# Opening loads in one queue, a second attention and turn bank, and earlier due times for batch 1

## The chip, the cores and the metric

One core of a Trainium2 chip. TensorE (PE) multiplies, VectorE (DVE) and ScalarE (ACT) work element by element, GpSimd (POOL) and SyncE (SP) issue loads and stores here. The metric is device time in microseconds, median of the runs.

## The reference

Linear attention with the map phi(x) = elu(x) + 1, then a mixture of four dense experts with given probabilities, over 8 batches of 8 heads, 576 rows and 64 channels (4608 tokens of 512 channels, 1024 hidden).

```python
q_p, k_p = (phi(q), phi(k))
kv = np.einsum('bhsd,bhse->bhde', k_p, v)
z = np.sum(k_p, axis=2)
num = np.einsum('bhsd,bhde->bhse', q_p, kv)
den = np.einsum('bhsd,bhd->bhs', q_p, z)[..., None] + 1e-06
...
p = domain_probs / (domain_probs.sum(-1, keepdims=True) + 1e-09)
for e in range(E):
    h = np.maximum(x @ w1[e], 0.0)
    out += p[:, e:e + 1] * (h @ w2[e])
```

## The kernel before, in words

**Tiles.** Heads are taken in pairs (two heads of 64 channels fill 128 partitions), four pairs per batch. Of a batch's 576 rows the first 512 are its main block (four chunks of 128); the last 64, the rests, of two batches share 128 partitions. After attention, x of the 512 main rows is one block j = 0 to 7; the rests of all batches make block 8.

**Attention of one pair** (`attention`, L302): k and q are mapped by an Exp on ACT (L332) and two operations on DVE (L324, L325), v is cast on ACT (L328). PE turns q with the identity (L342, and L345 for the rests' part) into the bank `tbank` (l2b3); ACT copies the turned q out (L353), DVE its rests' part (L355). PE forms key times value over the main rows (L364) and the rests (L367) into the bank `at`, ACT copies it (L377, L378), PE multiplies it with the turned q (L388), first three chunks, then the fourth and the rests, both in `at`, and DVE divides each by its denominator (L399, L401, L408). So a pair needs the mapped rests (`rest_maps`, L280: Exp L292, cast L295, DVE L289 and L290), once per batch. For batch 0, PE also turns x (`turn_x`, L485, into l2b3) and DVE copies it (L490). From batch 2 on the turns are DMA transposes issued by SP (L358).

**Experts.** Block 0 is done plainly: `first_l1` (L495: 32 products of 512 columns per expert) and `first_l2` (L505: 32 more). Expert 0's first layer is the wide form: six of the eight columns of hidden units are summed in six banks (l1b0 to 2, l2b0 to 2) as each pair's x arrives, the other two after. The other 64 units (8 blocks x 2 halves x 4 experts) use seven products of quarter blocks in place of eight (L649 and L757; expert 3's first layer is plain, L705). For that, sums of weight quarters are formed on DVE once (`sums_w1` L445, `sums_w2` L468), and each unit's scaled x (ACT, L607) is turned by a DMA transpose of SP (L609).

**Loads.** POOL issues pairs 1 to 3 of batch 0, all of batch 1 and the 32 weight loads (fp32 in HBM, cast to fp16 on the way), in program order. SP issues pair 0 and the rests of batch 0, the probabilities, and everything from batch 2 on. The pairs of batches 0 and 1 have three stage buffers in turn (two of their own, and w and m2, which the units use later); so pair (1,3) is loaded where pair (1,0) was.

**Order.** Every step is handed to a planner (`Plan`, L21) with engine, assumed duration, due time, keys that it reads and writes, and for loads an assumed transfer time (`move`). `order` (L55) plays the steps through: of those that are ready on the engine that is free first, the one with the earliest due time goes next; POOL keeps program order; a step is ready `HOP` after what it depends on. The result is the fixed order of instructions on each engine: on the chip each engine waits at the head of its own list, whatever is ready behind it. The planner's keys only set the order; waits on the chip follow from the tiles. A due time of a unit is `U(n)` = 84 + 6.4 n; batch 1's pairs are due at 47, 56, 65 and 72 (L847 to L858).

Of the kernel before, what the change touches and what calls it, by code (L numbers as in the profile page):

```python
# [20 lines left out]
class Plan:  # L21
# [6 lines left out]
    HOP = 0.2  # L28
# [7 lines left out]
    def add(self, eng, dur, pri, fn, r=(), w=(), move=0.0, after=0.0):  # L36
        n = len(self.ops)
        deps = set()
        for key in r:
            if key in self.wr:  # L40
                deps.add(self.wr[key])
            self.rd.setdefault(key, []).append(n)
        for key in w:
            if key in self.wr:
                deps.add(self.wr[key])
            deps.update(x for x in self.rd.get(key, ()) if x != n)
        for key in w:
            self.wr[key] = n
            self.rd[key] = []
        self.ops.append(  # L50
            dict(eng=eng, dur=dur, pri=pri, fn=fn, deps=deps, move=move, after=after)
        )
        return n
# [56 lines left out]
def kernel(  # L110
# [94 lines left out]

    def stage_keys(i):
# [6 lines left out]
    def dma(queue, pri, out_, in_, w, move, r=()):  # L213
        eng = nc.gpsimd if queue == "POOL" else nc.sync
        pl.add(
            queue,
            0.7 if queue == "POOL" else 0.45,
            pri,
            lambda: eng.dma_start(out=out_, in_=in_),
            r=r,  # L220
            w=w,
# [5 lines left out]
    def load_pair(b, pr, queue, pri):  # L227
# [5 lines left out]
        for t, o, key in ((k, kqs[i][:, 0], kk[0]), (v, vss[i], kk[2]), (q, kqs[i][:, 1], kk[1])):  # L233
            dma(queue, pri, o, t[b, hs, 0:NT].rearrange("h (p c) d -> p h c d", c=C), (key,), 0.82)

    def load_rest(b, queue, pri):
        par = b % 2
        rs = slice(par * R, par * R + R)
        for i, (t, o) in enumerate(((k, kqr[rs, 0]), (v, vr[rs]), (q, kqr[rs, 1]))):
            dma(queue, pri, o, t[b, :, NT:S].rearrange("h s d -> s h d"), (("str", par, i),), 0.6)  # L240

    def load_w1(e, dcs):
        for dc in dcs:
            dma("POOL", 0, w1_sb[e][:, dc, :], moe_w1[e, dc * P : (dc + 1) * P, :],
                (("w1", e, dc // 2, 0), ("w1", e, dc // 2, 1), ("w1c", e, dc)), 1.5)

    def load_w2(e):
        src = moe_w2[e].rearrange("(f p) d -> p f d", p=P)
        for c in range(0, FC, 2):
            i = c // HF  # L250
            dma("POOL", 0, w2_sb[e][:, c : c + 2, :], src[:, c : c + 2, :],
                (("w2", e, i, 0), ("w2", e, i, 1), ("w2c", e, c // 2)), 1.5)


    def probs():
# [24 lines left out]
    def rest_maps(b, pe_mode, pri):  # L280
# [7 lines left out]
        def maps():  # L288
            nc.vector.tensor_scalar(kqpr[rs], kqr[rs], 0.0, 1.0, AO.max, AO.add)  # L289
            nc.vector.tensor_tensor(out=kqpr[rs], in0=er[rs], in1=kqpr[rs], op=AO.min)  # L290

        pl.add("ACT", 1.15, pri, lambda: nc.scalar.activation(er[rs], kqr[rs], AF.Exp),  # L292
               r=(s_[0], s_[2]), w=ek)
        pl.add("ACT", 0.65, pri + 0.1,
               lambda: nc.scalar.copy(vprs[par][rs, :, 0:D], vr[rs]), r=(s_[1],), w=(("vpr", par),))  # L295
        pl.add("DVE", 1.8, pri + 0.5, maps, r=(s_[0], s_[2]) + ek, w=("kpr", "qpr"))
# [5 lines left out]
    def attention(b, pr, pe_mode, pri, step):  # L302
# [28 lines left out]
        for i in order_:  # L331
            pl.add("ACT", 0.65, pri + i * step, lambda i=i: nc.scalar.activation(  # L332
# [3 lines left out]
            if i == 0:  # L336
                pl.add("ACT", 0.62, pri + step, vcast, r=(sk[2],), w=(("vp", vi),))
        if pe_mode:

            def turn():  # L340
                for c in range(C):
                    nc.tensor.transpose(  # L342
                        out=tbank[:, c * P : (c + 1) * P], in_=qp[:, c], identity=identh
                    )
                nc.tensor.transpose(  # L345
                    out=tbank[:, NT : NT + R],
# [28 lines left out]
        def kvcopy():  # L375
            pkv = slot[0].rearrange("p (h e) -> p h e", h=2)
# [4 lines left out]
               r=(("kqp", pi, 0), ("vp", vi), ("vpr", par), "kpr"), w=("at",))  # L381
        pl.add("ACT", 0.45, pri + 4.5 * step, kvcopy, r=("at",), w=(("kvz", zi),))
# [13 lines left out]
        def norm(c0, n, ri):  # L396
            nd = at[:, 0 : n * 2 * DE].rearrange("p (c h e) -> p c h e", c=n, h=2)
# [17 lines left out]
        for u, (c0, n) in enumerate(((0, 3), (3, 2))):  # L415
            ri = rot("rc", 2)
            pl.add("PE", 0.06 * n, pri + (5 + u) * step, lambda c0=c0, n=n: nd_mm(c0, n),
                   r=(("qT", ti), ("qTr", par, pr), ("kvz", zi)), w=("at",))
            pl.add("DVE", (0.72, 0.75)[u], pri + (5.5 + u) * step,
                   lambda c0=c0, n=n, ri=ri: norm(c0, n, ri), r=("at",),  # L420
# [14 lines left out]

    def sums_w1(e, pri):
# [4 lines left out]
        K = lambda i, kk: ("w1", e, kk, i)  # L441
# [6 lines left out]
        for o, a, b_, alu, r, w in (  # L448
            (w1x[e][:, 2], q00, q01, AO.add, (K(0, 0), K(0, 1)), (X(2),)),
            (w1x[e][:, 1], q10, q11, AO.add, (K(1, 0), K(1, 1)), (X(1),)),  # L450
            (w1x[e][:, 0], q00, q11, AO.add, (K(0, 0), K(1, 1)), (X(0),)),
            (q10, q10, q00, AO.subtract, (K(0, 0),), (K(1, 0),)),
            (q01, q01, q11, AO.subtract, (K(1, 1),), (K(0, 1),)),
        ):
            pl.add("DVE", 0.75, pri, two(o, a, b_, alu), r=r, w=w)
        pl.add("DVE", 0.4, pri, lambda: nc.vector.tensor_scalar(q00, q00, -1.0, None, AO.mult),
               r=(), w=(K(0, 0),))

    def sums_w2(e, pri):
# [3 lines left out]
        K = lambda i, j: ("w2", e, i, j)  # L463
# [7 lines left out]
        for o, a, b_, r, w in (  # L471
            (t[0], qd(0, 1), qd(0, 0), (K(0, 1), K(0, 0)), T(0)),
            (t[1], qd(1, 1), t[0], (K(1, 1), T(0)), T(1)),
            (t[2], qd(1, 1), qd(0, 1), (K(1, 1), K(0, 1)), T(2)),
            (qd(0, 1), qd(1, 0), t[1], (K(1, 0), T(1)), K(0, 1)),
        ):
            pl.add("DVE", 0.75, pri, two(o, a, b_), r=r, w=(w,))


    def turn_x(pr, pri):  # L480
# [9 lines left out]
        pl.add("DVE", 0.45, pri + 0.5, lambda: nc.vector.tensor_copy(xt0[:, pr, :], tbank[:, 0:NT]),  # L490
# [22 lines left out]
    def w1k(e, dc, fj):  # L513
        return (("w1", e, dc // 2, fj // HF), ("w1c", e, dc))

    def w2k(e, fj):
        return (("w2", e, fj // HF, 0), ("w2", e, fj // HF, 1), ("w2c", e, fj // 2))

    def first_l1(e, pri, step, wide):
        ht = []  # L520
        banks = [(l1b[i], ("l1b%d" % i)) for i in range(3)]
        if wide:
            banks += [(l2b[i], ("l2b%d" % i)) for i in range(3)]
        ht = [rot("ht", len(hts)) for _ in range(FC)]

        def relu(fj, bank, key, pr_):
            pl.add("ACT", 0.6, pr_, lambda: nc.scalar.activation(hts[ht[fj]], bank, AF.Relu),
# [3 lines left out]
        if wide:  # L531
            for dc in range(DC):
                for fj in range(6):
                    bank, key = banks[fj]
                    p_ = pri + (dc * 6 + fj) * step
# [5 lines left out]
            done = 6  # L541
# [14 lines left out]
    def first_l2(e, ht, pri, step, wide):  # L556
# [17 lines left out]
        for i, (c, fjs, bi) in enumerate(parts):  # L574
            bank, key = l2b[bi], "l2b%d" % bi
# [4 lines left out]
            pl.add("PE", 0.216 * len(fjs), p_,  # L580
                   lambda c=c, fjs=fjs, bank=bank: mm2(e, ht, c, fjs, bank), r=r, w=(key,))
            if fjs[-1] == FC - 1:
                pl.add("DVE", 0.69, p_ + 1.0, lambda c=c, bank=bank: post(c, bank),
                       r=(key, "pnat"), w=(("ot", c // 2, c % 2),))
# [8 lines left out]
    def prep(n):  # L593
# [5 lines left out]
        for c in range(2):  # L599
# [7 lines left out]
            pl.add("ACT", 0.65, pri, lambda c=c, src=src, ps=ps: nc.scalar.activation(  # L607
# [23 lines left out]
    def l1_seven(n):  # L631
# [11 lines left out]
        K = lambda i, kk: ("w1", e, kk, i)  # L643
        X = lambda i: ("w1x", e, i)

        def prod(bank, wt, r, start):
# [14 lines left out]
            (A, ka, w1x[e][:, 2], X(2), xT[:, 1, 2:4], t_, True),  # L661
            (Bk, kb, w1x[e][:, 1], X(1), xT[:, 0, 0:2], t_, True),
# [268 lines left out]
```

## Time and profile before

| | us |
|---|---|
| median of 3 runs | 562.05 (557.68 to 563.96) |
| the profiled execution | 562.97 |
| its span in the profile | 561.2 |
| PE busy | 498.4 (89%) |
| DVE busy | 413.5 (74%) |
| ACT busy | 335.7 (60%) |
| POOL busy | 38.9 (7%) |

How to read the rows below. A stretch row has its bounds, its length, then the busy time of PE, PEld (TensorE's loads of the stationary operand, beside PE), DVE, ACT and POOL with the number of instructions, the mean granted clock of TensorE (1.00 is full speed), the mean busy share of the 16 DMA engines and the GB/s moved. A timeline row has the start, the length, the engine, the line of the kernel and the operation, what it writes and reads, its shape and the count merged into it; in brackets the idle time of the engine ahead of it and what ended that. SPq and POOL rows with DMA_DIRECT2D are issues of loads, not transfers. A wait row has the waiting engine and line, what ended the wait, the total, the number and the longest.

### The profile page before, as it was taken

The page shows a single profiled execution, that of the slowest core. Times are in us where ns is not written, and L with a number is a line of the kernel's source. Part 1 is how long each engine was busy: PE and PEld are TensorE (multiplying, and loading weights), DVE is VectorE, ACT ScalarE, POOL GpSimd, SP SyncE. Part 2 cuts the span into 40 slices and gives each one's busy share as a digit, 9 for nine tenths or more (in the row PEclk, how much of TensorE's full clock was granted, in tenths as well). Part 3 has the DMA queues.
Part 4 walks back from the last instruction along what each step waited for, and adds up shares of the span by engine and source line. Part 5 has one row for each costly group of instructions (what it writes and reads, how often), then busy time and mean ns, then how long its engine had stood idle before and what let it go on. Part 6 is the DMA issues. An engine that isn't in the chain of part 4 may idle for free.

```text
span 561.2 us, 13887 instructions
## 1 busy us (share of the span) xinstructions
PE 498.4 (89%) x5624; PEld 427.8 (76%) x5624; DVE 413.5 (74%) x993; ACT 335.7 (60%) x617; POOL 38.9 (7%) x62
## 2 busy tenths in 40 slices
PE   0067979578999999999999999999999999999994
PEld 0033434235899999999999999999999999999993
DVE  2175565847969888988888898889897775757662
ACT  2143345488547965895687678756854674656431
POOL 7545030000000000000000000000000000000000
PEclk9998998889999999999999999999999999999998
DMA  9999328398535745693668447564434242523211
GB/s 226 231 216 233 73 73 143 110 201 180 144 48 148 167 107 143 116 219 69 127 146 170 112 112 147 146 138 119 86 68 86 39 95 43 92 39 77 39 40 39
DMA packets 126929, 67.44 MB, mean 120 GB/s; under 512 B 97520, under 2 KB 120816, under 8 KB 126864
## 3 DMA queue, kind: packets, MB, share of 16 engines
q1 hardware_dynamic: 118384, 52.26, 43.0%
q0 software_dynamic: 8480, 14.29, 12.2%
q8 instruction: 44, 0.72, 0.5%
q14 instruction: 21, 0.17, 0.1%
HBM read 45.16 MB, written 9.44 MB: 97 GB/s over the span
## 4 chain that ended last, share of the span: by engine, by line
PE 83%; DVE 6%; DMA 6%; ACT 2%; issue 2%; POOL 1%; DVEq 0%; ACTq 0%; POOLq 0%
PE l2b L757 33%; PE l1b L649 25%; PE l1b L705 10%; PE l1b L495 6%; DMA w<-in_moe_w_dram 5%; PE l2b L505 3%; PE at L388 2%; PE at L364 1%; DVE x L401 1%; DVE ot L562 1%; DMA xT<-xp 1%; PE l2b L495 1%; DVE rc L399 1%; DVE kqp L324 1%; DVE kqp L325 0%
## 5 line engine op out<-in xcount | busy, mean ns | idle before, releaser
L649 PE MATMUL l1b<-xs,w 128*128 128x128 f16 x1536 | 114.8, 219 | 1.5 <-ACT h L686 0.9
L757 PE MATMUL l2b<-w,h 128*128 128x256 f16 x768 | 112.3, 273 | 0.8 <-DVE h L693 0.8
L757 PE MATMUL l2b<-t,s 128*128 128x256 f16 x768 | 111.1, 273 | 0.0
L649 PEld LDWEIGHTS <-w 128*128 128x128 f16 x1536 | 99.6, 98 | 5.4 <-issue 1.8
L757 PEld LDWEIGHTS <-s 128*128 128x128 f16 x1024 | 93.6, 98 | 8.1
L607 ACT ACTIVATE xp<-x,p_nat 128x512 f16<-128x512 f16 x112 | 75.2, 716 | 7.5 <-DMA xT<-xp 7.2
L649 PEld LDWEIGHTS <-w1x 128*128 128x128 f16 x1152 | 74.9, 98 | 4.6 <-issue 2.0
L757 PEld LDWEIGHTS <-h 128*128 128x128 f16 x768 | 69.9, 98 | 7.1 <-DVE h L693 1.1
L705 PE MATMUL l1b<-xT,w 128*128 128x256 f16 x512 | 74.2, 273 | 0.0
L743 DVE TENSOR_TENSOR s<-h 128x512 f16<-128x512 f16 x128 | 53.7, 420 | 26.7 <-ACT h L724 26.2
L724 ACT ACTIVATE h<-l1b 128x512 f16<-128x512 f32 x64 | 38.2, 596 | 43.2 <-PE l1b L705 35.6
L649 PE MATMUL l1b<-xT,w1x 128*128 128x128 f16 x768 | 57.6, 219 | 0.0
L625 DVE TENSOR_TENSOR xs<-xT 128x256 f16<-128x256 f16 x144 | 49.2, 375 | 9.9 <-PE l1b L649 5.9
L705 PEld LDWEIGHTS <-w 128*128 128x128 f16 x512 | 49.6, 98 | 5.6
L683 ACT ACTIVATE h<-l1b 128x512 f16<-128x512 f32 x48 | 28.6, 596 | 33.7 <-PE l1b L649 33.3
L332 ACT ACTIVATE ek<-kq 128x512 f16<-128x512 f32 x60 | 37.3, 627 | 14.2 <-DVE kqpr L290 7.4
L689 DVE CUSTOM_DVE_ANT_0 h<-l1b,w 128x512 f16<-128x512 f32 x48 | 33.0, 687 | 16.2 <-PE l1b L649 7.8
L675 ACT ACTIVATE l1b<-l1b 128x512 f32<-128x512 f32 x48 | 28.0, 583 | 23.6 <-PE l1b L649 20.2
L757 PE MATMUL l2b<-w,s 128*128 128x256 f16 x256 | 38.4, 273 | 0.0
L680 DVE TENSOR_TENSOR w<-l1b,m 128x512 f32<-128x512 f32 x48 | 33.0, 687 | 7.2 <-PE l1b L649 4.7
L324 DVE TENSOR_SCALAR kqp<-kq 128x512 f16<-128x512 f32 x60 | 25.5, 424 | 15.8 <-PE at L364 11.8
L693 DVE CUSTOM_DVE_ANT_0 h<-l1b,w 128x512 f16<-128x512 f32 x48 | 33.0, 689 | 4.1 <-PE l1b L649 2.2
(89 smaller groups left out, 627.3 us busy)
## 6 DMA issues: line engine op xcount, KB each, us to landing
w<-in_moe_w_dram POOLq DMA_DIRECT2D x32, 256.0 KB, 8.9
out_dram<-ot SPq DMA_DIRECT2D x16, 512.0 KB, 2.9
kq<-in_k_dram SPq DMA_DIRECT2D x25, 256.0 KB, 3.2
vs<-in_v_dram SPq DMA_DIRECT2D x25, 256.0 KB, 3.1
kq<-in_q_dram SPq DMA_DIRECT2D x25, 256.0 KB, 3.1
kq<-in_k_dram POOLq DMA_DIRECT2D x5, 256.0 KB, 8.0
vs<-in_v_dram POOLq DMA_DIRECT2D x5, 256.0 KB, 8.0
kq<-in_q_dram POOLq DMA_DIRECT2D x5, 256.0 KB, 7.4
```

The costliest lines, as they stand in the source:

```text
L332: pl.add("ACT", 0.65, pri + i * step, lambda i=i: nc.scalar.activation(ek[:, i], kq[:, i], AF.Exp), r=(sk[i],), w=(("ek", ei, i),))
L495: nc.tensor.matmul(out=bank, lhsT=w1_sb[e][:, dc, fj * P : (fj + 1) * P], rhs=xt0[:, dc, :], start=(dc == 0), stop=(dc == DC - 1),)
L607: pl.add("ACT", 0.65, pri, lambda c=c, src=src, ps=ps: nc.scalar.activation(xp[:, c, :], src, AF.Copy, scale=ps), r=r, w=(("xp", xi, c),))
L625: lambda o=o, a=a, b_=b_, alu=alu: tt(out=o, in0=a, in1=b_, op=alu),
L649: nc.tensor.matmul(out=bank[:, fc * P : (fc + 1) * P], lhsT=wt[:, kc, fc * P : (fc + 1) * P], rhs=r[:, kc, :], start=(start and fc == 0 an ...
L680: pl.add("DVE", 0.69, p_ + 1.5, lambda: nc.vector.tensor_tensor(out=w, in0=W, in1=m2_b, op=AO.subtract), r=(kw, ("m2",)), w=(("w", wi),))
L689: pl.add("DVE", 0.69, p_ + 0.5, lambda: nc.vector._custom_dve(TENSOR_ADD_SAT, out=hq(n, 1, 1), in0=A, in1=w, s0=BIG, s1=0.0), r=(ka, ("w", ...
L693: pl.add("DVE", 0.69, p_ + 0.5, lambda: nc.vector._custom_dve(TENSOR_ADD_SAT, out=hq(n, 0, 0), in0=Bk, in1=w, s0=BIG, s1=0.0), r=(kb, ("w" ...
L705: nc.tensor.matmul(out=ph[:, f2 * 2 * P : (f2 + 1) * 2 * P], lhsT=w1_sb[e][:, dc, (2 * fp + f2) * P : (2 * fp + f2 + 1) * P], rhs=xT[:, :, ...
L724: lambda ph=ph, f=f, c0=c0: nc.scalar.activation(h[:, :, f, c0 : c0 + 2, :], ph.rearrange("p (c u t) -> p u c t", c=2, u=2), AF.Relu), r=( ...
L743: pl.add("DVE", 0.42, U(n + 1) + d - 0.5, lambda i=i, a=a, b_=b_, alu=alu: tt(out=s4[:, i], in0=a, in1=b_, op=alu), r=r, w=(Q(i),))
L757: nc.tensor.matmul(out=l2b[bank][:, half * HD : (half + 1) * HD], lhsT=a[:, c, :], rhs=w[:, c], start=(opens and first and c == 0), stop=( ...
```

## The change

The diff, cut to what changes the order of work (durations of other steps are set 0.07 to 0.13 lower throughout; reads and writes of weight slices are named per slice loaded instead of per pair of slices):

- The rests of batch 0 are loaded by POOL, ahead of its other loads; the probabilities by POOL too, behind the last first-layer weights of expert 0. The identity is made ahead of all loads; part of the memsets becomes steps of the planner.
- Loads of batch 2, and the rests of batch 3, wait for the landing of the last weight load (the mark).
- In batch 0's pairs, key times value and the second part of the product with the turned q go to two parts of the bank l2b2; the turn of q goes to l2b1, that of x stays in l2b3. The wide form has four banks instead of six. ACT instead of DVE copies the turned x.
- Batch 1's pairs are due at 36, 45, 53 and 58. The weight sums of the first layer are not planned ahead of 22.

```diff
-    HOP = 0.2
+    HOP = 0.28
@@ dma: a load can set the mark, or wait for it
-    def dma(queue, pri, out_, in_, w, move, r=()):
+    last = {}
+    def dma(queue, pri, out_, in_, w, move, r=(), hold=False, mark=False):
+        def go():
+            i = eng.dma_start(out=out_, in_=in_)
+            if mark:
+                last["mark"] = i.ins.name
+            if hold:
+                tc.add_manual_dep(i.ins, last["mark"], ..., reason="load order")
-            0.7 if queue == "POOL" else 0.45,
+            0.72 if queue == "POOL" else 0.5,
@@ load_pair, load_rest, load_w1, load_w2
-            dma(queue, pri, o, t[b, hs, 0:NT]..., (key,), 0.82)
+            dma(queue, pri, o, t[b, hs, 0:NT]..., (key,), 0.7, hold=b == 2)
-            dma(queue, pri, o, t[b, :, NT:S]..., (("str", par, i),), 0.6)
+            dma(queue, pri, o, t[b, :, NT:S]..., (("str", par, i),), 0.75, hold=b in (2, 3))
-                (("w1", e, dc // 2, 0), ("w1", e, dc // 2, 1), ("w1c", e, dc)), 1.5)
+                (("w1", e, dc, 0), ("w1", e, dc, 1)), 1.4)
-                (("w2", e, i, 0), ("w2", e, i, 1), ("w2c", e, c // 2)), 1.5)
+                (("w2", e, c // 2, 0), ("w2", e, c // 2, 1)), 1.55, mark=(e, c) == (3, 6))
@@ probs
-        dma("SP", 6, raw, ..., ("praw",), 1.0)
+        dma("POOL", 6, raw, ..., ("praw",), 1.5)
-            dma("SP", 6, rrest[par * R : (par + 1) * R], ..., (("prawr", par),), 0.3)
+            dma("POOL", 6, rrest[par * R : (par + 1) * R], ..., (("prawr", par),), 0.4)
@@ rest_maps: one DVE step for k and q becomes two
-        pl.add("DVE", 1.8, pri + 0.5, maps, r=(s_[0], s_[2]) + ek, w=("kpr", "qpr"))
+        for i, key in enumerate(("kpr", "qpr")):
+            pl.add("DVE", 0.92, pri + 0.5, lambda i=i: maps(i), r=(s_[0], s_[2]) + ek, w=(key,))
@@ attention
-    def attention(b, pr, pe_mode, pri, step):
+    def attention(b, pr, pe_mode, pri, step, two=False):
+            tq, tk = (l2b[1].bitcast(FP16), "l2b1") if two else (tbank, "l2b3")
+        kvs_, ndk = slot[0], (("at",), ("at",))
+        nds = [slot[0:3], slot[0:2]]
+        if two:
+            more = [l2b[2][:, i * 2 * DE : (i + 1) * 2 * DE] for i in range(3)]
+            kvs_, ndk = more[0], (("at",), ("l2b2n",))
+            nds[1] = more[1:3]
+        kvk = ("l2b2k",) if two else ("at",)
@@ turn_x
-        pl.add("DVE", 0.45, pri + 0.5, lambda: nc.vector.tensor_copy(xt0[:, pr, :], tbank[:, 0:NT]),
+        pl.add("ACT", 0.5, pri + 0.5, lambda: nc.scalar.copy(xt0[:, pr, :], tbank[:, 0:NT]),
@@ first_l1 (wide): 3 + 1 banks
-            banks += [(l2b[i], ("l2b%d" % i)) for i in range(3)]
+            banks += [(l2b[i], "l2b%d" % i) for i in range(1)]
-                for fj in range(6):
+                for fj in range(4):
-            done = 6
+            done = 4
@@ sums_w1
-            pl.add("DVE", 0.75, pri, two(o, a, b_, alu), r=r, w=w)
+            pl.add("DVE", 0.62, pri, two(o, a, b_, alu), r=r, w=w, after=22)
@@ the opening's order
-    consts()
+    make_identity(nc, identh)
+    nc.vector.memset(kqpr, 0.0)
+    consts(0)
+    pl.add("DVE", 0.8, 5, lambda: consts(1), w=(("vp", 1), ("vpr", 1), ("kvz", 1)))
+    for i in range(2):
+        pl.add("DVE", 0.27, 6 + 30 * i, lambda i=i: nc.vector.memset(qTr[i], 0.0),
+               w=[("qTr", i, pr) for pr in range(DC)])
     load_pair(0, 0, "SP", 0)
-    load_rest(0, "SP", 1)
-    probs()
+    load_rest(0, "POOL", 0)
     load_pair(0, 1, "POOL", 0)
     load_w1(0, (0,))
     load_pair(0, 2, "POOL", 0)
     load_w1(0, (1,))
-    pl.add("POOL", 2.0, 0, lambda: make_identity(nc, identh), w=("ident",))
     for pr in range(DC):
         if pr == 3:
             load_pair(0, 3, "POOL", 0)
             load_w1(0, (2, 3))
-        attention(0, pr, True, 2.5 + 4.2 * pr, 0.5)
-        turn_x(pr, 6 + 4.2 * pr)
+            probs()
+        attention(0, pr, True, 2.5 + 4 * pr, 0.4, two=True)
+        turn_x(pr, 6 + 4 * pr)
-    rest_maps(1, True, 47)
-    attention(1, 0, True, 47, 0.8)
+    rest_maps(1, True, 36)
+    attention(1, 0, True, 36, 0.8)
-    attention(1, 1, True, 56, 0.8)
+    attention(1, 1, True, 45, 0.8)
-    attention(1, 2, True, 65, 0.8)
+    attention(1, 2, True, 53, 0.8)
-    attention(1, 3, True, 72, 0.8)
+    attention(1, 3, True, 58, 0.8)
```

## Rows read from the trace of the kernel before

**Rows 1.** Stretches: us; busy PE, PEld, DVE, ACT, POOL (count); clock, DMA, GB/s

```profile
0.00:27.96 27.96, 0.76 (x5) 0.45 (x5) 6.78 (x21) 6.07 (x9) 17.75 (x31) 1.00 1.09 229
27.96:53.11 25.15, 16.82 (x91) 9.22 (x91) 15.76 (x49) 8.44 (x20) 14.01 (x21) 1.00 1.15 220
...
57.73:141.60 83.87, 66.21 (x401) 33.77 (x400) 55.63 (x125) 49.28 (x94) 6.35 (x9) 0.92 0.58 126
...
160.00:474.00 314.00, 313.22 (x3952) 293.24 (x3950) 266.26 (x650) 218.32 (x405) 0.00 (x0) 1.00 0.54 117
474.00:561.20 87.20, 79.17 (x969) 73.38 (x967) 52.93 (x115) 40.54 (x69) 0.00 (x0) 0.98 0.28 56
```

**Rows 2.** Timeline to 28 us: start, length, engine, line, out<-in, [idle before <-releaser]

```profile
1.76 0.47 SPq L219 DMA_DIRECT2D kq<-in_q_dram  x1
...
2.83 0.74 POOL L219 DMA_DIRECT2D kq<-in_q_dram  x1
...
3.73 0.64 SPq L219 DMA_DIRECT2D kqr<-in_q_dram  x1
...
7.35 0.29 POOL masks.py:199 TENSOR_SCALAR_AFFINE_SELECT identh<-identh 128x128 f16<-128x128 f16 x1
...
8.63 0.43 DVE L324 TENSOR_SCALAR kqp<-kq 128x512 f16<-128x512 f32 x1 [3.75 <-DMA kq<-in_q_dram]
...
19.30 1.06 ACT L292 ACTIVATE ek<-kqr 64x1024 f16<-64x1024 f32 x1 [4.40 <-DMA kqr<-in_q_dram]
...
24.95 0.29 DVE L265 TENSOR_REDUCE prs<-praw 128x32 f32<-128x128 f32 x1 [15.23 <-DMA praw<-in_moe_domain_probs_dram]
...
27.06 0.68 DVE L290 TENSOR_TENSOR kqpr<-ek,kqpr 64x1024 f16<-64x1024 f16 x1
...
27.96 0.62 PE L364 MATMUL at<-vp,kqp 128*128 128x130 f16 x4
```

**Rows 3.** Page: queues (packets, MB, share); issues (count, KB, us to landing)

```profile
q1 hardware_dynamic: 118384, 52.26, 43.0%
q0 software_dynamic: 8480, 14.29, 12.2%
...
kq<-in_q_dram SPq DMA_DIRECT2D x25, 256.0 KB, 3.1
...
kqr<-in_q_dram POOLq DMA_DIRECT2D x1, 128.0 KB, 10.4
```

**Rows 4.** Timeline of PE, third pair of batch 0

```profile
40.71 0.59 PE L364 MATMUL at<-vp,kqp 128*128 128x130 f16 x4
...
43.27 1.49 PE L495 MATMUL l2b<-s,w 128*128 128x512 f16 x3
...
45.95 0.27 PE L388 MATMUL at<-kvz,qT 128*128 128x130 f16 x1 [0.88 <-DVE x L401]
...
47.12 0.59 PE L364 MATMUL at<-vp,kqp 128*128 128x130 f16 x4
```

**Rows 5.** Waits over the span: us in total, times, longest us

```profile
POOL kq L219 <- DVE kqp L325: 28.2, 2, 24.6
...
PE at L388 <- DVE x L401: 9.4, 10, 1.8
...
DVE qTr L355 <- ACT qT L353: 5.3, 5, 1.8
```

**Rows 6.** Timeline of PE, first-layer blocks of experts 1 to 3

```profile
64.64 7.07 PE L495 MATMUL l1b<-s,w 128*128 128x512 f16 x32
...
84.30 8.46 PE L495 MATMUL l1b<-s,w 128*128 128x512 f16 x32
...
114.41 8.77 PE L495 MATMUL l1b<-s,w 128*128 128x512 f16 x32
```

**Rows 7.** Costliest groups on the page: count, busy us, mean ns, idle before

```profile
L693 DVE CUSTOM_DVE_ANT_0 h<-l1b,w 128x512 f16<-128x512 f32 x48 | 33.0, 689 | 4.1 <-PE l1b L649 2.2
```

**Rows 8.** Waits of PE from 160 us to the end

```profile
PE l1b L649 <- ACT l1b L675: 0.8, 2, 0.4
```

More of the change, by code (lines that the diff above doesn't have):

```diff
@@ L50, in add @@
         self.ops.append(
[L51 removed]
+            dict(eng=eng, dur=dur, pri=pri, fn=fn, deps=deps, move=move, after=after, w=w)
         )
@@ L204, in rot, with lk @@
         return i % n
+    def lk(i):
+        return ("l2b2k", "l2b2n") if i == 2 else ("l2b%d" % i,)
     def stage_keys(i):
@@ L210, in stage_keys @@
         return ("w", 0), ("w", 1), ("m2",)
-    def dma(queue, pri, out_, in_, w, move, r=()):
+    last = {}
+    def dma(queue, pri, out_, in_, w, move, r=(), hold=False, mark=False):
         eng = nc.gpsimd if queue == "POOL" else nc.sync
+        def go():
[3 more added lines that the diff above has]
+            if hold:
+                tc.add_manual_dep(
+                    i.ins,
+                    last["mark"],
+                    mybir.DependencyInfo(
+                        mybir.DependencyClass.Sync, mybir.DependencyReason.DATA
+                    ),
+                    reason="load order",
+                )
         pl.add(
             queue,
-            0.7 if queue == "POOL" else 0.45,
+            0.72 if queue == "POOL" else 0.5,
             pri,
-            lambda: eng.dma_start(out=out_, in_=in_),
-            r=r,
-            w=w,
+            go,
+            r=r + (("mark",) if hold else ()),
+            w=w + (("mark",) if mark else ()),
             move=move,
@@ L233, in load_pair @@
         for t, o, key in ((k, kqs[i][:, 0], kk[0]), (v, vss[i], kk[2]), (q, kqs[i][:, 1], kk[1])):
-            dma(queue, pri, o, t[b, hs, 0:NT].rearrange("h (p c) d -> p h c d", c=C), (key,), 0.82)
+            dma(queue, pri, o, t[b, hs, 0:NT].rearrange("h (p c) d -> p h c d", c=C), (key,), 0.7, hold=b == 2)
     def load_rest(b, queue, pri):
@@ L331, in attention @@
         for i in order_:
-            pl.add("ACT", 0.65, pri + i * step, lambda i=i: nc.scalar.activation(
+            pl.add("ACT", 0.55, pri + i * step, lambda i=i: nc.scalar.activation(
                 ek[:, i], kq[:, i], AF.Exp), r=(sk[i],), w=(("ek", ei, i),))
@@ L394, in nd_mm, with norm @@
                 )
-        def norm(c0, n, ri):
-            nd = at[:, 0 : n * 2 * DE].rearrange("p (c h e) -> p c h e", c=n, h=2)
+        def norm(u, c0, n, ri):
+            nd = at[:, 0 : n * 2 * DE]
+            if two and u:
+                nd = l2b[2][:, 2 * DE : 6 * DE]
+            nd = nd.rearrange("p (c h e) -> p c h e", c=n, h=2)
             rc = rc_b[ri]
@@ L574, in first_l2 @@
         for i, (c, fjs, bi) in enumerate(parts):
-            bank, key = l2b[bi], "l2b%d" % bi
+            bank, key = l2b[bi], lk(bi)
             p_ = pri + i * step * (8 / len(parts))
@@ L720, in l1_plain @@
                        lambda ph=ph, fp=fp, f2=f2: prod(ph, fp, f2),
-                       r=(("xT", ti),) + tuple(("w1", e, kk, (2 * fp) // HF) for kk in range(2)),
+                       r=(("xT", ti),) + k1(e, (2 * fp) // HF, 0) + k1(e, (2 * fp) // HF, 1),
                        w=(key,))
-            pl.add("ACT", 0.62, U(n) + 1.6 * fp + 1.5,
+            pl.add("ACT", 0.52, U(n) + 1.6 * fp + 1.5,
                    lambda ph=ph, f=f, c0=c0: nc.scalar.activation(
@@ L779, in l2_unit @@
                    lambda bank=bank, half=half, a=a, w=w, opens=opens: prod(bank, half, a, w, opens),
-                   r=(ak, wk), w=("l2b%d" % bank,))
+                   r=(ak,) + wk, w=lk(bank))
         if not last:
@@ L898 @@
     ):
-        for o in pl.order():
+        todo = pl.order()
+        for o in todo:
             o["fn"]()
```

157 lines of the change are left out of this document (79 added, 78 removed).

## Prediction

> **What bounds the kernel now.** I read the busy time by stretch first [rows 1]. From 160 to 474 us TensorE is busy 313.22 of 314 us, and after 160 us it has 0.8 us of waits that the trace can name [rows 8]. There the kernel is bound by TensorE's own work, the same before and after; nothing is to be had but a loss. The 87.2 us at the end hold 8 us without TensorE, mostly the last sums and stores, untouched by the change. What is open lies ahead of 160 us, in three stretches of rows 1: 0 to 27.96 us, where TensorE works 0.76 us; 27.96 to 53.11 us, batch 0's four head pairs, busy 16.82 of 25.15; and 57.73 to 141.60 us, where the four experts' plain blocks for batch 0 run beside the attention of batch 1, busy 66.21 of 83.87.
>
> Next I read the timeline of the first stretch, looking for what comes last ahead of the first key-value product at 27.96 us [rows 2]. Pair 0 is there early: its last load was issued at 1.76 and used at 8.63 us. The rests are late: the query rests, issued on SP at 3.73, let the Exp of L292 start at 19.30, 15.6 us later. But that Exp was done at 20.36 and DVE mapped the rests only up to 27.74. In between DVE stood at L265 for the probabilities (it idled 15.23 us, until 24.95), with the maps queued behind it in its fixed order. So two things in series hold the opening: a slow rest load, then a blocked DVE.
>
> Then the timeline of one pair [rows 4]: key-value products start at 40.71 and 47.12, a period of 6.41 us, in which PE waits 0.88 us at L388 until DVE has normalised the first three chunks out of the one attention bank.
>
> Last the waits: POOL, which issues all weights, stood 24.6 us in one piece for a stage buffer of batch 1 that pair (1,0) held [rows 5]. That is the due time of batch 1, not DMA, holding back the last six weight loads.
>
> **The change, part by part.** The sum is made against the profiled execution, 562.97 us (span 561.2 and 1.8 outside); the median of the runs is 562.05, 0.9 lower.
>
> *Rests and probabilities on POOL.* Today POOL's third load is issued at 2.83 us [rows 2]. The three rests take those three places, behind the identity (its second operation takes 0.29, I count 0.6 for both), so the query rests are issued at 3.4. Their landing on this queue so early is not in the trace. Bounds: 3.1 us, the median of SP's query loads, and 10.4 us, that of batch 1's query rests, issued on POOL in the thick of the weights [rows 3]. I take the 6.9 us of pair 0's query load [rows 2], the nearest in time: landing at 10.3 (6.5 to 13.8). Exp 1.06; the maps, now four half operations for two of 0.68, 1.6; 0.3 for hand-overs: mapped at 13.3 instead of 27.74, **a gain of 14.4** (18.2 to 10.9). The reduce of the probabilities no longer stands ahead, provided the planner, which prices their landing itself, puts it behind pair 0. Every load behind the rests on POOL is issued three issues (some 2.1 us) later, and those behind the probabilities another three; what hides it is that POOL, by the order in the code, had issued 26 of 32 weight loads when it stalled for 24.6 us [rows 5].
> Why should another queue help? The two queues' packets on the page: POOL's queue moved 14.29 MB in 8,480 packets, 1.7 KB each, SP's 52.26 MB in 118,384, 0.44 KB each [rows 3]. Small pieces on SP beside large ones on POOL came through in 15.6 us; in POOL's own line they stand ahead of the large ones. The Trainium skill (DMA: Bandwidth & Descriptors, "Issuing engines are not separate DMA queues") says that loads from any engine end on the same 16 DMA engines and interleave, so that moving an issue saves sequencer time only. By that rule the rests would land no earlier and the sum of this step would be 5.5 in place of 14.4.
>
> *Two attention and two turn banks.* The second normalisation has its own bank, so the 0.88 us wait goes from each of four pairs. Of the wide first-layer products two columns of six go: of the three on l2b in 1.49 us [rows 4] two, 0.99 per pair, come after the last pair instead, eight products at 7.07/32 = 0.22, or 1.8 [rows 6]. Gain 4 x 1.87 - 1.8 = **5.7**. The next pair's key-value product shares a bank with the second normalisation; the rows show DVE's L355 waiting 5.3 us in all for ACT's L353, the other reader of its bank [rows 5], so I count no overlap there. Ends: nothing, if the freed time becomes a wait on ACT or DVE; and 9.4, where the stretch shrinks to DVE's own 15.76 us [rows 1]. The turned x moves from DVE to ACT, four copies; ACT is busy 8.44 us of 25.15 there.
>
> *Batch 1 more urgent.* In the third stretch TensorE stands 83.87 - 66.21 = 17.7 us, and two of its 32-product blocks took 8.46 and 8.77 instead of 7.07 us, 3.1 more [rows 1, 6]: 20.8 to win. POOL's stall goes when pair (1,0) is mapped 11 planner units sooner. What is late next: the chain of each pair of batch 1 through ACT and DVE, which TensorE meets in a fixed order. I take half, **10.4**, since the row gives no reason for either end, 0 or 20.8. DVE's 55.63 us would fit the shortest stretch of 63.1.
>
> *Free or nearly so.* Memsets put later and the probabilities' arithmetic: DVE is busy 6.78 of 27.96 us; without that cover, some 2 us. Finer names of weight slices and the earliest time of the weight sums only order DVE. The hold puts all of batch 2's loads, and on SP whatever is queued behind them (the turning loads of the first unit), behind the last weight; that weight comes earlier than it did with the stall gone, and batch 2 is first needed eight units on. If the stall stayed, SP would wait too.
>
> Sum: 562.97 - 14.4 - 5.7 - 10.4 = 532.5; less 0.9 for the median, **532**.
>
> **Rivals.** *Rests no faster.* They still share the engines with POOL's other loads and SP's pair 0, and are used at 19.30; only the block by the probabilities is gone: mapped at 19.3 + 1.06 + 1.6 + 0.3 = 22.3, a gain of 5.5, so 541.4. For it: on POOL itself a rest took 10.4 us. Against it: the packet sizes. The Trainium skill's rule above says this.
> *The middle gives nothing back.* TensorE meets batch 1's chains as unready as today, only earlier: 562.97 - 20.1 = 542.9. For: ten waits of L388 on the normalisation are in the trace [rows 5], and batch 0's four pairs have one each, so six lie here. Against: the 24.6 us stall, which is plainly removed.
> *Slower: the units are dealt anew.* The planner's hop goes from 0.2 to 0.28 and DVE's 512-column operations from 0.69 to 0.62, while the trace has 689 ns for them [rows 7]. All 64 units are interleaved from these; DVE is busy 85% there [rows 1]. If TensorE then waits for DVE or ACT in each unit, it decides at 30.5/64 = 0.48 us per unit; at 0.6 us the time is 532.5 + 38.4 = 571. Against: two waits of 0.4 us in 400 us say that there is room.
> *It doesn't do what it says:* the probabilities land late on POOL and DVE stands there again. Then step one falls to nothing, 546.9.
>
> **Numbers.** The forecast, all three steps in part or whole, 0.62; rests no faster 0.12; middle gives nothing 0.12; DVE blocked again 0.05; units dealt anew 0.06; better than all steps' middles by over 16 us 0.03. All steps at their good end give 514.6, at their bad end 552.1; leaving out the corners, the range is 516 to 549. About 1% (5.6 us) can be told from no change: faster takes all but the units and the pairing of two bad rivals: 0.89, same 0.05, slower 0.06.
>
> **What would show it.** L292 near 11 us and the first L364 near 13 to 14; the reduce L265 with little idle ahead of it; a pair's period near 4.5 us with no wait of L388 on the first normalisation; no POOL wait of over 5 us; first L757 near 110 instead of 141.6; PE still busy over 99% from there on. I am wrong if DVE still idles over 5 us for a load ahead of the maps, if the rests' landing is over 12 us, or if PE has new waits beyond the opening.

## The result, and the profile after

The changed kernel takes 514.8 us (median of 4 runs, 513.35 to 516.54) where the kernel before takes 561.32 on the same chip: a ratio of 0.9177, 95% interval 0.9115 to 0.9238. The profiled execution took 514.07 us, its span is 512.2. The gain of 46.5 us is half as much again as the 30 forecast, and the time lies 1.2 us below the range. Ratios here and below leave out runs that lie over 1.5% above the fastest of the same kernel; only e4 has such runs.

Busy time by stretch of the changed kernel, with the columns of [rows 1]. The cuts are the same events: first product with the rests, start of expert 0's second layer, first second-layer product of the units (now L799), and two cuts in the units.

```profile
0.00:10.51 10.51, 0.59 (x4) 0.43 (x5) 5.03 (x18) 4.97 (x7) 8.97 (x18) 1.00 0.83 203
10.51:32.02 21.51, 16.54 (x104) 9.22 (x105) 17.91 (x54) 14.74 (x32) 15.88 (x24) 1.00 1.15 242
32.02:91.25 59.23, 56.92 (x355) 29.43 (x353) 48.58 (x107) 37.79 (x74) 17.91 (x27) 1.00 1.00 221
...
160.00:430.00 270.00, 270.00 (x3401) 252.84 (x3399) 226.12 (x557) 184.94 (x346) 0.00 (x0) 1.00 0.52 114
430.00:512.20 82.20, 74.26 (x905) 68.80 (x903) 51.03 (x111) 37.24 (x64) 0.00 (x0) 0.97 0.24 54
```

The second of them in the kernel before, between the same cuts:

```profile
27.96:57.73 29.77, 21.44 (x104) 10.95 (x104) 17.83 (x52) 12.08 (x27) 14.81 (x22) 0.94 1.15 229
```

Against [rows 1], TensorE (second number) reaches the first cut at 10.51 us for 27.96 (there the whole key-value product waited, here only its rests' part); expert 0's second layer starts at 32.02 for 57.73; the next stretch lasts 59.23 us for 83.87. From 160 to 430 us TensorE is busy 270.00 of 270, as full as before. The whole gain lies ahead of the units.

The opening, in the timeline: the issue of the query rests, their Exp, PE's product with them (was L367) and the end of their maps. They answer to the rows of L292, L290 and L364 in [rows 2].

```profile
3.15 0.69 POOL L224 DMA_DIRECT2D kqr<-in_q_dram  x1
...
8.95 1.06 ACT L314 ACTIVATE ek<-kqr 64x1024 f16<-64x1024 f32 x1
...
10.51 0.29 PE L400 MATMUL l2b<-vpr,kqpr 128*128 128x130 f16 x1 [4.56 <-DVE kqpr L312]
...
11.05 0.42 DVE L312 TENSOR_TENSOR kqpr<-ek,kqpr 64x512 f16<-64x512 f16 x1
```

The Exp starts 5.8 us after the issue, for 15.6 before, and the maps end at 11.47 for 27.74. The reduce of the probabilities, with no idle time ahead of it, comes when DVE has nothing older to do:

```profile
23.53 0.28 DVE L286 TENSOR_REDUCE prs<-praw 128x32 f32<-128x128 f32 x1
```

The pairs of batch 0 on PE (L397 was L364, L421 was L388), answering to [rows 4]:

```profile
13.18 0.64 PE L397 MATMUL l2b<-vp,kqp 128*128 128x130 f16 x4
...
18.17 0.64 PE L397 MATMUL l2b<-vp,kqp 128*128 128x130 f16 x4
...
19.98 0.40 PE L397 MATMUL l2b<-vp,kqp 128*128 128x130 f16 x4
...
20.27 0.33 PE L527 MATMUL l2b<-identh,x 128*128 128x128 f16 x3
...
21.17 0.33 PE L421 MATMUL at<-kvz,qT 128*128 128x130 f16 x3
21.84 0.22 PE L421 MATMUL l2b<-kvz,qT 128*128 128x130 f16 x1 [0.34 <-ACT kvz L411]
...
22.64 0.82 PE L537 MATMUL l1b<-s,w 128*128 128x512 f16 x3
```

The third and fourth pairs' key-value products (18.17 and 19.98) lie 1.8 us apart for 6.41; the two before them (13.18 and 18.17) lie 5.0 apart. The fourth chunk (21.84, into l2b) waits 0.34 us for ACT's copy and not for the normalisation of the first three.

The same rows correct the clock column, which reads 1.00 from 10.51 to 32.02 us here and from 27.96 to 53.11 in [rows 1]. The four key-value products take 0.64 us at 18.17 and 0.40 at 19.98. Before, three products of 512 columns take 1.49 us at 43.27 [rows 4] and, in the next pair:

```profile
49.62 0.81 PE L495 MATMUL l2b<-s,w 128*128 128x512 f16 x3
```

So TensorE ran at the lower of its two levels (1.2 GHz) up to about 49 us in the kernel before and up to about 19 us in the changed one, and at the higher (2.4 GHz) behind that, but for the stretches in which the column shows less.

All waits of POOL over 1.5 us in total, its last weight issues, and PE's longest waits in the whole span, in that order (for [rows 5] and [rows 8]):

```profile
POOL w L224 <- DMA w<-in_moe_w_dram: 3.8, 7, 0.8
POOL w L224 <- issue: 1.8, 2, 1.7
```

```profile
57.77 2.11 POOL L224 DMA_DIRECT2D w<-in_moe_w_dram  x3 [1.66 <-issue]
```

```profile
PE l2b L397 <- ACT vp L351: 5.4, 1, 5.4
PE l2b L400 <- DVE kqpr L312: 4.6, 1, 4.6
PE l1b L691 <- ACT h L725: 1.4, 1, 1.4
```

The 24.6 us stall is gone: the last weights are issued at 57.77 us and after. Of PE's waits over 1.5 us, only the two of the first 10.5 us are left.

### The profile page after: what moved, and what is told of

It is laid out like the page before. It is cut to its first block, busy times and chain, and to the rows that moved or that the text cites. A ratio compares the mean times of both kernels' runs of the same rounds, so it can differ in the third digit from the quotient of the medians.

```text
span 512.2 us, 13906 instructions
## 1 busy us (share of the span) xinstructions
PE 486.8 (95%) x5624; PEld 424.3 (83%) x5624; DVE 411.8 (80%) x1005; ACT 333.7 (65%) x621; POOL 42.8 (8%) x68
## 4 chain that ended last, share of the span: by engine, by line
PE 90%; DVE 3%; ACT 2%; DMA 2%; issue 1%; POOL 0%; POOLq 0%; DVEq 0%; ACTq 0%
PE l2b L799 37%; PE l1b L691 28%; PE l1b L747 11%; PE l2b L547 5%; PE l1b L537 5%; PE at L421 2%; PE at L397 1%; DMA vr<-in_v_dram 1%; DMA xT<-xp 1%; DVE x L437 0%; ACT ek L355 0%; ACT xp L649 0%; PE l2b L367 0%; PE at L400 0%; DVE ot L839 0%
## 5 line engine op out<-in xcount | busy, mean ns | idle before, releaser
L691 PE MATMUL l1b<-xs,w 128*128 128x128 f16 x1536 | 116.0, 219 | 1.4 <-ACT h L725 1.4
L799 PE MATMUL l2b<-t,s 128*128 128x256 f16 x768 | 114.6, 273 | 0.1
L799 PE MATMUL l2b<-w,h 128*128 128x256 f16 x768 | 113.6, 273 | 0.2 <-DVE h L731 0.2
L799 PEld LDWEIGHTS <-s 128*128 128x128 f16 x1024 | 92.5, 98 | 7.8 <-DVE s L785 0.3
L649 ACT ACTIVATE xp<-x,p_nat 128x512 f16<-128x512 f16 x112 | 76.5, 719 | 3.4 <-DMA xT<-xp 3.2
L799 PEld LDWEIGHTS <-h 128*128 128x128 f16 x768 | 69.5, 98 | 6.4 <-DVE h L731 0.3
L731 DVE CUSTOM_DVE_ANT_0 h<-l1b,w 128x512 f16<-128x512 f32 x48 | 32.9, 686 | 10.4 <-ACT h L728 5.0
L799 PE MATMUL l2b<-w,s 128*128 128x256 f16 x256 | 38.4, 273 | 0.0
L348 DVE TENSOR_TENSOR kqp<-ek,kqp 128x512 f16<-128x512 f16 x64 | 27.2, 426 | 9.0 <-ACT ek L355 5.2
```

The costliest lines, as they stand in the source:

```text
L649: pl.add("ACT", 0.55, pri, lambda c=c, src=src, ps=ps: nc.scalar.activation(xp[:, c, :], src, AF.Copy, scale=ps), r=r, w=(("xp", xi, c),))
L691: nc.tensor.matmul(out=bank[:, fc * P : (fc + 1) * P], lhsT=wt[:, kc, fc * P : (fc + 1) * P], rhs=r[:, kc, :], start=(start and fc == 0 an ...
L731: pl.add("DVE", 0.62, p_ + 0.5, lambda: nc.vector._custom_dve(TENSOR_ADD_SAT, out=hq(n, 1, 1), in0=A, in1=w, s0=BIG, s1=0.0), r=(ka, ("w", ...
L799: nc.tensor.matmul(out=l2b[bank][:, half * HD : (half + 1) * HD], lhsT=a[:, c, :], rhs=w[:, c], start=(opens and first and c == 0), stop=( ...
```

## The experiments

Each kernel ran in three rounds beside the kernel before, whose median was 560.76 to 561.74 us; a gain is told against the median of the same rounds, a loss against the 514.8 of the changed kernel, whose runs spread from 513.35 to 516.54. "Undone" starts from the changed kernel, "alone" from the kernel before.

| kernel | us | ratio to before, 95% interval |
|---|---|---|
| changed | 514.80 | 0.9115 to 0.9238 |
| e1: old names | 533.23 | 0.9472 to 0.9543 |
| e2: old due times | 520.04 | 0.9224 to 0.9303 |
| e3: new names alone | 549.14 | 0.9712 to 0.9824 |
| e4: new due times alone | 557.38 | 0.9765 to 0.9941 |
| e5: rests on SP again | 521.21 | 0.9235 to 0.9307 |
| e6: probabilities on SP again | 516.22 | 0.9146 to 0.9230 |
| e7: one bank of each kind | 520.69 | 0.9230 to 0.9304 |
| e8: no hold | 514.57 | 0.9119 to 0.9192 |
| e9: old durations and hop | 517.09 | 0.9183 to 0.9268 |
| e10: loads on POOL alone | 549.63 | 0.9757 to 0.9846 |
| e11: rests first on SP | 519.44 | 0.9235 to 0.9300 |
| e12: hop 0.2 | 518.18 | 0.9211 to 0.9286 |
| e13: names and loads | 529.29 | 0.9379 to 0.9469 |
| e14: names, loads, due times | 521.52 | 0.9242 to 0.9340 |
| e15: rests and probabilities on SP | 520.73 | 0.9231 to 0.9314 |

**The third stretch: names or due times (e1 to e4).** The theory I formed on seeing the result came from the planner's own book, the times at which it expects things when it lays out the order:

```
kernel                          planner expects the last weight at
before                          135.1
before, new names alone (e3)     79.5
changed, old names (e1)         121.2
changed                          73.3
```

In the old names a first-layer load writes a name shared with its neighbour, and a second-layer load too; the planner takes that for an order and holds every second load until the one ahead has landed. On the chip nothing holds them: before, the last six went out from 80.94 us on, and that late only because of the stage buffer. The last of them was issued at 84.2 us, and none of POOL's loads took over 12.0 us to land, so all weights were there by 97 us.

What such a book does to the order can be read on TensorE. First the kernel before, the last two pairs of batch 1; then the changed kernel, one pair of batch 1:

```profile
105.95 0.34 PE L388 MATMUL at<-kvz,qT 128*128 128x130 f16 x3 [1.21 <-ACT qT L353]
...
109.41 0.62 PE L364 MATMUL at<-vp,kqp 128*128 128x130 f16 x4 [1.90 <-DVE kqp L325]
...
114.24 0.27 PE L388 MATMUL at<-kvz,qT 128*128 128x130 f16 x1 [1.82 <-DVE x L401]
```

```profile
55.71 1.90 PE L537 MATMUL l1b<-s,w 128*128 128x512 f16 x8
57.45 0.33 PE L421 MATMUL at<-kvz,qT 128*128 128x130 f16 x3
57.62 1.89 PE L537 MATMUL l1b<-s,w 128*128 128x512 f16 x8
59.34 0.22 PE L421 MATMUL at<-kvz,qT 128*128 128x130 f16 x1
```

Before, the steps of the two pairs stand alone, each waiting for ACT or DVE, and the first-layer block of expert 3 comes behind them at 114.41 [rows 6], though its weights had landed. In the changed kernel, pieces of the blocks stand between the steps of a pair and cover these waits.

```diff
-  (("w1", e, dc, 0), ("w1", e, dc, 1))                    # load_w1
+  (("w1", e, dc // 2, 0), ("w1", e, dc // 2, 1), ("w1c", e, dc))
-  (("w2", e, c // 2, 0), ("w2", e, c // 2, 1))            # load_w2
+  (("w2", e, c // HF, 0), ("w2", e, c // HF, 1), ("w2c", e, c // 2))
```

> The changed kernel with the weight slices named as before: two loads write a common name, so that the planner holds every second one back until the one ahead of it has landed. Nothing else differs, and POOL issues the same loads in the same order. Theory 'names' (the third stretch shrank because the planner now expects the weights in time): the stretch from expert 0's second layer to the first L799 goes from 59 back to over 80 us, and the time to 538 to 552. Rival 'due times' (what the prediction said): the names order little, 514 to 518.

Measured 533.23, 18.4 us lost. The stretch from expert 0's second layer to the first L799:

```profile
34.63:107.77 73.14, 62.58 (x358) 31.18 (x357) 46.66 (x100) 36.82 (x70) 16.34 (x25) 0.91 0.65 138
```

It is 13.9 us longer than the 59.23 of the changed kernel, and TensorE stands 10.6 us in it for 2.3, at a mean granted clock of 0.91 for 1.00. The direction is that of "names", but both of its sizes were missed: 73 us for over 80, and 533 for 538 to 552. The rival's 514 to 518 falls. Loads and readers were renamed together, in e1 and in e3; which of the two matters was not tried apart.

```diff
-  rest_maps(1, True, 36); attention(1, pr, True, 36 / 45 / 53 / 58, 0.8)
+  rest_maps(1, True, 47); attention(1, pr, True, 47 / 56 / 65 / 72, 0.8)
```

> The changed kernel with batch 1 due at 47, 56, 65 and 72 again. 'Names': at most 8 us slower, 516 to 523. 'Due times': the third stretch loses what it won, some 23 us, 534 to 540.

Measured 520.04: 5.2 lost, as "names" expected. The same stretch of it, 7.2 us longer:

```profile
32.93:99.32 66.39, 59.45 (x364) 31.89 (x363) 52.06 (x118) 42.16 (x81) 17.67 (x27) 0.95 0.96 226
```

> The kernel before with only the new names of the weight slices; loads, banks, due times and durations as before. 'Names': a gain of 20 us or more, 532 to 541. 'Due times': 558 to 563, no change.

The edit is that of e1 reversed, in the kernel before. Measured 549.14, a gain of 12.6, between the two expectations. The stretch, and POOL's longest wait (10.8, the last number):

```profile
61.10:126.62 65.52, 60.22 (x364) 32.36 (x363) 48.53 (x107) 40.62 (x79) 6.16 (x9) 0.95 0.57 133
```

```profile
POOL kq L219 <- DVE kqp L324: 15.0, 2, 10.8
```

The stretch is 18.4 us shorter than the 83.87 of before with due times untouched, and the longest stall for a stage buffer is 10.8 us for 24.6. What is missing of 20 was lost outside: the second layer of expert 0 starts at 61.10 for 57.73. Why is open.

> The kernel before with only batch 1's due times of 36, 45, 53 and 58. 'Names': no more than 3 us won, 558 to 562, since the weights are still expected late. 'Due times': the forecast's 10.4 us or more, 540 to 551.

Measured 557.38, a gain of 4.4 by the medians, but the four runs spread from 549.52 to 558.89, and by the ratio the gain is 8.3, with an interval from 3 to 13. By time alone e4 settles little. POOL's longest wait, in its profiled execution of 558.43:

```profile
POOL kq L219 <- DVE kqp L325: 29.7, 2, 25.4
```

The due times alone leave the stall as it was. That is the point where the prediction's third step had its reason wrong. What sets the spread is open.

**The opening: queue, block and banks (e5 to e7, e10, e11, e15).**

```diff
-    load_rest(0, "POOL", 0)        # e5
+    load_rest(0, "SP", 1)
```

> The changed kernel with batch 0's rests issued by SP behind pair 0, as before; the probabilities stay on POOL. 'Packets' (small pieces come through late beside POOL's large ones): the Exp of the rests starts at 15 us or later instead of 8.95, and 6 to 10 us of that reach the end, 520 to 525. 'Same engines' (a load is no earlier for its queue): the Exp starts within 1.5 us of where it did, 513 to 517.

Measured 521.21, 6.4 lost, inside "packets". The issue of the query rests, DVE's use of pair 0's last load, and the Exp:

```profile
3.73 0.64 SPq L224 DMA_DIRECT2D kqr<-in_q_dram  x1
...
9.00 0.43 DVE L347 TENSOR_SCALAR kqp<-kq 128x512 f16<-128x512 f32 x1 [4.29 <-DMA kq<-in_q_dram]
...
16.79 1.06 ACT L314 ACTIVATE ek<-kqr 64x1024 f16<-64x1024 f32 x1 [3.86 <-DMA kqr<-in_q_dram]
```

Behind pair 0 on SP the query rests come 13.1 us after their issue; on POOL, in the changed kernel, they were in use after 5.8.

```diff
-    load_pair(0, 0, "SP", 0); load_rest(0, "POOL", 0)        # e11
+    load_rest(0, "SP", 0); load_pair(0, 0, "SP", 0)
```

> The changed kernel with the rests on SP, but ahead of pair 0 rather than behind it. 'Place in line' (what delays a load is what stands ahead of it on its own queue): the Exp of the rests starts by 9.5 us, 513 to 517. 'Packets' (small pieces lose against POOL's large ones wherever they stand on SP): the Exp starts after 11 us, 517 to 522.

Neither as expected: the Exp is early, as "place in line" said, and the time is 519.44, as "packets" said. The issue of the third and the last of SP's six loads, the Exp, and the uses of pair 0's v and q:

```profile
2.22 0.64 SPq L224 DMA_DIRECT2D kqr<-in_q_dram  x1
...
4.07 0.47 SPq L224 DMA_DIRECT2D kq<-in_q_dram  x1
...
8.70 1.05 ACT L314 ACTIVATE ek<-kqr 64x1024 f16<-64x1024 f32 x1
...
13.73 0.63 ACT L351 CAST vp<-vs 128x512 f16<-128x512 f32 x1 [2.65 <-DMA vs<-in_v_dram]
...
15.58 0.43 DVE L347 TENSOR_SCALAR kqp<-kq 128x512 f16<-128x512 f32 x1 [3.26 <-DMA kq<-in_q_dram]
```

Now pair 0 is what comes late: its q, the sixth load, is used at 15.58 where the sixth load of e5 is used at 16.79. So it isn't the small piece that loses, but whatever stands last in SP's line of six while POOL loads beside it. The change cuts SP's line in half.

```diff
-        dma("POOL", 6, raw, ...); dma("POOL", 6, rrest[...], ...)        # e6
+        dma("SP", 6, raw, ...); dma("SP", 6, rrest[...], ...)
```

> The changed kernel with the probabilities issued by SP as before; the rests stay on POOL. 'DVE blocked': they land at 20 us or later, the reduce stands ahead of maps on DVE, which idles 5 us or more for it, 518 to 524. 'Not blocked' (the finer book puts the reduce behind what is ready): DVE idles under 2 us, 513 to 517.

Measured 516.22, "not blocked"; the 1.4 lost lie within the spread of the changed kernel. With the rests gone from SP, the probabilities issued there land in time:

```profile
2.27 0.48 SPq L224 DMA_DIRECT2D praw<-in_moe_domain_probs_dram  x1
...
11.77 0.27 DVE L286 TENSOR_REDUCE prs<-praw 128x32 f32<-128x128 f32 x1
```

> The changed kernel with both the rests and the probabilities on SP, in the old order. One at a time they cost 6.4 and 1.4 us. 'Two things in series' (a slow rest load, then DVE blocked for the probabilities): more than the sum, 525 to 530, with DVE idle 5 us or more for L286. 'Only the rests count': 521 to 523.

e5 and e6 together, in the old order. Measured 520.73, at the edge of "only the rests count". Maps of the rests and reduce of the probabilities on DVE, then PE's wait for the maps:

```profile
18.63 0.42 DVE L312 TENSOR_TENSOR kqpr<-ek,kqpr 64x512 f16<-64x512 f16 x1
...
26.00 0.28 DVE L286 TENSOR_REDUCE prs<-praw 128x32 f32<-128x128 f32 x1
```

```profile
PE l2b L400 <- DVE kqpr L312: 12.7, 1, 12.7
```

The probabilities are nearly as late as before (19.3 us from issue to landing, for 20.5), but their reduce stands behind the maps and blocks nothing. So the block by DVE belonged to the order of before, and the new order is free of it with either queue.

> The kernel before with only the rests and the probabilities of batch 0 moved to POOL as in the change. The prediction's first step by itself is 14.4 us. 'It carries through': the first product with rests at 11 to 14 instead of 27.96 us, and 545 to 550. 'Given back': as early, but the later order, laid out for late weights, waits again, 554 to 560.

The change's loads in the kernel before, alone. Measured 549.63, a gain of 11.1: "it carries through" at its weak end. PE's first product with the rests is 17.2 us earlier (11.19 for 28.37), but expert 0's second layer only 12.0 (45.73 for 57.73), and the stretch behind it is as long as before:

```profile
45.73:130.24 84.51, 66.95 (x401) 34.12 (x400) 55.63 (x125) 49.32 (x93) 12.14 (x18) 0.90 0.72 159
```

```diff
-        attention(0, pr, True, 2.5 + 4 * pr, 0.4, two=True)        # e7
+        attention(0, pr, True, 2.5 + 4 * pr, 0.4)
```

> The changed kernel with one attention bank and one turn bank in batch 0's pairs; the wide form keeps its four banks. 'Banks carry step two' (it measured 9.4 us): the pairs' period goes from 4.3 back to over 6 us, and 7 to 10 us reach the end, 521 to 525. 'Clock and loads carry it' (the pairs are merely earlier and their loads there): under 3 us, 514 to 518.

Measured 520.69, 5.9 lost, a little under the range of "banks". From the first product with rests to expert 0's second layer, PE's wait for the normalisation, and three products of the wide form:

```profile
10.97:41.13 30.16, 20.41 (x104) 10.26 (x105) 21.92 (x60) 14.59 (x33) 21.32 (x33) 0.89 1.15 241
```

```profile
PE at L421 <- DVE x L437: 4.2, 4, 1.5
```

```profile
35.47 1.44 PE L537 MATMUL l1b<-s,w 128*128 128x512 f16 x3 [0.67 <-DMA kq<-in_k_dram]
```

30.16 us for 21.51: 8.7 lost there. Of these, 4.8 are idle time of TensorE (9.8 for 5.0), and the four waits of [rows 4], 4.2 us, are back. The other 3.9 are busy time: 20.41 us for 16.54 with the same 104 products, of which more run at the lower clock (three take 1.44 us at 35.47, and 0.82 at 22.64 in the changed kernel). Some 3 us are won again behind.

**Hold, durations, hop (e8, e9, e12).**

> The changed kernel without the hold: batch 2's loads and the rests of batches 2 and 3 go as soon as their buffers are free. The prediction priced the hold at nothing: 513 to 517. Rival 'the hold clears the opening': early loads of batch 2 share the engines with the weights, and its maps crowd DVE and ACT, so the last weight load lands 4 us or more later and the time is 518 to 524.

Edit: `hold` left out of both loads. Measured 514.57, no difference. The price of nothing was right.

> The changed kernel planned with the durations, the hop of 0.2 and the transfer times of before; names, loads, banks, due times and hold as changed. 'Costs matter little': 514 to 518. 'Costs carry the rest' (the single undoings so far sum to 37 of 46.5 us): 522 to 526.

Edit: hop, durations and transfer times as in the kernel before. Measured 517.09, 2.3 lost, hardly outside the changed kernel's spread: they matter little.

> The changed kernel with the planner's hop at 0.2 instead of 0.28, all else as changed; an attempt at a faster one. 'Hop is slack in the order': instructions are placed closer than the chip hands over, PE gets new waits, 515 to 518. 'Hop too long': the opening tightens, 511 to 514.

Edit: `HOP = 0.2`. Measured 518.18, 3.4 slower: no faster kernel. Its units:

```profile
160.00:430.00 270.00, 268.93 (x3364) 250.70 (x3362) 227.07 (x563) 184.26 (x344) 0.00 (x0) 1.00 0.53 115
```

TensorE stands 1.07 us in them for 0.00. Of the rest, 1.7 us are lost in batch 0's pairs (10.63 to 33.81, so 23.2 us for 21.5). That a shorter hop makes the order too tight fits this, but was not shown apart.

**Do they add (e13, e14).**

> The kernel before with two parts of the change: the new names of the weight slices and the opening's loads on POOL. Alone they won 12.6 and 11.1 us. 'They add' (one ends the first stretch, the other the third): 536 to 540. 'They overlap' (both buy the same wait): 545 to 549.

Measured 529.29, a gain of 32.2 where the two alone give 23.7: more than either expectation. Expert 0's second layer starts at 40.13, and then:

```profile
40.13:105.40 65.27, 59.91 (x365) 31.90 (x364) 49.34 (x109) 40.42 (x78) 15.39 (x23) 0.95 0.87 199
```

The names give the third stretch (65.27, as in e3). The loads give the first; ahead of the third the names now help too: expert 0's second layer starts 5.6 us sooner than with the loads alone, where by themselves they lost 3.4.

> The same with batch 1's due times of 36 to 58 as well; alone they won 4.4 us. 'Due times work only on a true book' (with the names right, the planner can place batch 1 early): 7 to 11 us below the kernel with names and loads. 'They add': 4 to 5 us below it.

Measured 521.52, 7.8 below e13: "only on a true book". The stretch is 7.0 shorter than in e13:

```profile
40.35:98.58 58.23, 57.42 (x364) 30.00 (x363) 47.21 (x105) 39.86 (x78) 15.08 (x23) 1.00 0.93 209
```

So names, loads and due times together give 40.0 of the 46.5 us. The rest, 6.5, is about what the banks cost when undone (5.9); the banks, durations and hop (2.3 undone) were not tried beside these three.

## Why the prediction was wrong

Both sums are against the profiled executions: 562.97 - 514.07 = 48.9 us.

| step of the prediction | forecast | measured |
|---|---|---|
| rests and probabilities on POOL (maps done at 27.74, now 11.47) | 14.4 | 16.3 |
| two banks (from there to expert 0's second layer, 29.99, now 20.55) | 5.7 | 9.4 |
| batch 1 more urgent (to the first L757 or L799) | 10.4 | 24.6 |
| the rest of the span (419.6, now 420.9) | 0 | -1.3 |

**The step that failed** is the third, and with it the line on edits that are free: "Finer names of weight slices and the earliest time of the weight sums only order DVE." The names order all engines, since the planner lays out PE, DVE and ACT by when it expects the weights. e1 and e3 put 13.9 and 18.4 us of this stretch on them; the due times, to which the step gave all, are worth 7.0 of it on top of names and loads (e13 to e14), and 7.2 when undone (e2). The reason given, that the stall of POOL goes with earlier due times, is refuted by the trace of e4: 25.4 us with them.

The end of 20.8 that bounded the step was too low as well. It was 17.7 of idle time and 3.1 of two slow blocks. Of the idle time 15.4 went, which is within it. But TensorE's busy time fell by 9.3 (66.21 to 56.92), not by 3.1. A part is work carried out of the stretch: two pairs of batch 2 (L364: 28 products, now 20) and 24 unit products (L649: 88, now 64) lie behind it now. TensorE is busy 2.8 us longer there, and that rest of the span is 1.3 us longer. The other 6.5 us are the same products in less time; the mean granted clock of the stretch is 1.00 for 0.92. Over the whole span the same 5,624 products keep TensorE busy for 486.8 us instead of 498.4. So 11.6 of the 49 us are TensorE at work for a shorter time, a large part of it for the higher clock (how much was not measured apart). This step counted only the two blocks.

**The first step** found the right waits and was 1.9 us short, 1.1 of it since the rests came in 5.8 us, not 6.9. Of the two things in series, the slow load is confirmed (e5, 6.4 us; e10, 11.1 together with the probabilities) and the block of DVE was there before, but it went with the order, not with the queue (e15). My reason for the queue, small packets beside large ones, is refuted by e11: the same small loads are early when they stand first on SP. The Trainium skill (DMA: Bandwidth & Descriptors, "Issuing engines are not separate DMA queues") says that such a move saves sequencer time only. By that rule the rests would land no earlier. The runs differ: e5 loses 6.4 us. The query rests came 13.1 us after their issue as the sixth load of SP's line, and 5.8 to 6.5 us after it as the third load of POOL or SP (e11: issued at 2.22, in use at 8.70).

**The second step** was 3.7 us short. I took away one wait and two products; e7 loses 8.7 us in that stretch, with 3.9 us of longer busy time that the sum had no term for. The pairs also overlap, 1.8 us apart at the closest. I excluded that because the key-value product shares a bank with the second normalisation. It does go ahead (19.98), and the normalisation waits for it:

```profile
20.54 0.18 DVE L435 RECIPROCAL rc<-l2b 128x4 f32<-128x4 f32 x1 [0.47 <-PE l2b L400]
```

The wait is 0.47 us of DVE, less than the overlap brought.

**The rivals.** "Rests no faster", "the middle gives nothing back" and "DVE blocked again" all fail on the rows above. Of "the units dealt anew" nothing is seen in the changed kernel (270.00 of 270); in e12, with the shorter hop, the span behind the first L799 is 2 us longer, and not 0.5 us per unit. The case of a gain beyond all middles, which had 0.03, is what came. That the three good ends add up to 514.6, next to the measured time, is chance: the first step stayed below its end of 18.2 and the third went beyond its end of 20.8.

## What to carry to other kernels

Where an order is written ahead of time by a planner, its picture of what depends on what is a part of the kernel: a name too coarse for two independent loads left the chip waiting for an order laid out for weights that had long landed. Price an edit to such names by what the planner expects before and after, against when the trace shows the thing there. And don't take idle time as the bound of a gain where a new order can also carry work out of the stretch (2.8 us here) or let the same products run in less time (6.5 us). Where the clock column and the time of a known product disagree, go by the product.

## What was not expected of the hardware

SP's six opening loads, 3 of 256 KB and 3 of 128 KB, were through at about the same time in either order, with POOL loading beside them: last use at 16.79 us in e5, at 15.58 in e11. Which three were late went by their place. Three of them issued on POOL instead, ahead of its own loads, were in use 5.8 us after their issue.
